# Loop products of an attention kernel cut into 64-row, 32-column TensorE tiles, with the products against V split by row halves into one PSUM bank

## The chip, the cores and the metric

The kernel runs on one core of a Trainium2 chip. The metric is the device time of one execution in microseconds; lower is better. Each time is the median of several executions, and one further execution was recorded by the hardware profiler.

## What is computed

A transformer block with adaptive layer norm on a 2048 x 512 input: attention with 32 query heads of 16 elements that share one key and one value head, then a gated feed-forward layer of width 1792. The core of the reference:

```python
q = (x @ wq).reshape(B, S, H, Dh).transpose(0, 2, 1, 3)      # H = 32, Dh = 16
k = x @ wk
v = x @ wv
scores = jnp.einsum("bhqd,bkd->bhqk", q, k) * (Dh ** -0.5)
p = _softmax(scores, axis=-1)
o = jnp.einsum("bhqk,bkd->bhqd", p, v)                        # then @ wo
...
h = _sigmoid(x @ w_gate) * (x @ w_up)                         # then @ w_down
...
h = _layernorm(x, axis=-1) * (1 + ca) + sa                    # ca, sa, ga, ... from silu(c) @ w_mod
x = x + ga * _A_ref(h, A_wq, A_wk, A_wv, A_wo)
h = _layernorm(x, axis=-1) * (1 + cb) + sb
x = x + gb * _B_ref(h, B_w_gate, B_w_up, B_w_down)
```

## The kernel before

A **prologue** (`PLAN`, a hand-written order) loads the input, normalises it, and makes K (`kp`), V (`V`, fp32, with columns of ones so that row sums come with the product) and the first queries. A **loop** of 512 steps does all attention and seven eighths of the feed-forward layer. A **tail** does the last eighth.

The loop runs over 32 units (`units`: 8 blocks of 256 queries, each with 4 groups of 8 heads), and in each over 16 blocks of 128 keys. The query tile `qp` holds head pairs twice, in partitions 0 to 63 and 64 to 127 (index `j`), so score products have a contraction of 64 rows and two of them can stand in the two row halves of the TensorE array at once. A step s holds:

- four **`sa`** products (`a_tile`): scores with queries on the partitions, 64 x 128 tiles with 512 columns, for the row maxima. Each goes to one of three PSUM banks, and `a_max` on VectorE (DVE) reduces it into `mx`. They run about 1.3 units ahead (`A0 = 84`), since a unit's maxima enter its `qp` as two more rows (`max_rows`).
- four **`st`** products (`st_tile`): scores with keys on the partitions, 64 x 128 tiles with 512 columns, in one of two banks; ScalarE (ACT) takes the exponential into `P`.
- one **`pv`** for step s - 2 (`LAG`): four fp32 products of `V` (128 rows, 32 columns) with `P`, side by side in the four column groups of the array, accumulated over the unit's 16 steps in the one bank `c`. Where no side product is running, `pv` is cut into two halves of 256 columns at two places of the step.
- **side products**: queries (`pq`), the output projection (`po`), gate and up (`pgu`, 256 columns), down (`pd`), in fp16 with hi and lo parts. `Couple` runs two groups at once, one in each row half, and swaps the halves in the middle so that each group sees all 128 rows. `plan`, `places` and `piece` deal a couple's terms into three places of a step, `RATE = 4.5` terms a step.

The order on TensorE, VectorE and ScalarE in the loop is the order of the code (`keep_in_program_order`). The step's skeleton:

```python
scores(0); piece() or light(s); scores(1)      # scores(n): st_tile, then a_tile
pv(*vq[0], None if full else 0)
scores(2); piece(); scores(3)
if not full: pv(*vq[0], 1)
piece()
```

`unit_end` copies the finished bank `c` to `cs`, on DVE for all but the first four units.

Of the kernel before, what the change touches and what calls it, by code (L numbers as in the profile page):

```python
# [22 lines left out]
QB = 512  # L23
# [3 lines left out]
NKB = S // P  # L27
# [29 lines left out]
LAG = 2  # L57
# [4 lines left out]
SKIP = 9  # L62
GAP = 2
KEPT = 2
RATE = 4.5
MOST = 6
WSTEPS = 110
WLAST = 112
WLATE = 2
WSTORE = 5  # L70
QPLAIN = 3
FIRST = 75
QLEAD = 6
W1 = 2
# [10 lines left out]
def adaln_mqa_glu_kernel(  # L85
# [34 lines left out]

    def sbank(name):
        return psum["s"].tile([P, 512], F32, tag=name, name=name, bufs=psum["banks"][name])

    def cbank(name):
        return psum["c"].tile([P, 512], F32, tag="c", name=name, bufs=1)


    class Ordered:
        def __init__(self, engine):
# [9 lines left out]

    class Group:
        def __init__(self, stage, n, name, term, end, begin=None, w=1):
# [17 lines left out]
    class Couple:  # L162
# [3 lines left out]
        def part(self, n0, n1):  # L166
            if n0 == 0:
                for g in self.gs:
                    g.open()
            m = self.gs[0].n  # L170
            for n in range(n0 * self.w, n1 * self.w):
                for j in range(2):
                    g = self.gs[j ^ (n >= m)]
                    l_, r_, *cut = g.term(n % m, slice(64 * j, 64 * j + 64))
                    pe.matmul(g.bank[:, cut[0]] if cut else g.bank, l_, r_, start=(n == 0), stop=(n == 2 * m - 1))
            if n1 == self.n:
                for k, g in enumerate(self.gs):
                    g.end(g.bank, k == 1)
# [366 lines left out]
    def a_product(i, n):  # L545
        qp = get_q(i)
        if i not in mxs:
            mxs[i] = wp.tile([P, 8, 2, 4], F32, tag="mx", name="mx", bufs=2)
        kc, qt, j, r = spot(n)
        sa = sbank("sa")  # L550
        pe.matmul(sa, qp[64 * j:64 * j + 64, r, qt * P:(qt + 1) * P],
                  kp[64 * j:64 * j + 64, kc * 512:(kc + 1) * 512], start=True, stop=True)
        return i, n, sa

    def a_max(i, n, sa):
        kc, qt, j, r = spot(n)
        dve.tensor_reduce(mxs[i][:, 4 * j + r, qt, kc:kc + 1], sa, axis=AX.X, op=ALU.max)
        if i > 0 and n == 63:
            pend.append((i,))

    def a_tile(i, n):
        a_max(*a_product(i, n))
# [26 lines left out]

    def st_tile(i, t, pr, j):  # L590
        qp = get_q(i)
        if j == 0:
            P_["p"] = P2.tile([P, 2, 512], F32, tag=f"P{pr}", name=f"P{pr}", bufs=PBUFS)
        p_ = P_["p"]
# [8 lines left out]
    def pv(i, t, half=None):  # L603
        if t == 0 and half != 1:
            Cs[i] = cbank("c")
        cut = slice(0, QB) if half is None else slice(half * QB // 2, (half + 1) * QB // 2)
# [3 lines left out]
        if half == 0:  # L610
            return
        for hh in range(4):
            del Ps[i, t, hh]
        if t == NKB - 1:
            unit_end(i)

    def unit_end(i):
        b, o = units[i]
        cs = t32("cs")
        if pinned and b > 0:  # L620
            dve.tensor_copy(cs, Cs.pop(i))
        else:
            act.activation(cs, Cs.pop(i), AF.Identity)
        if i == len(units) - 1:
            last.append(cs)
            return
        lD = dr.tile([2, 8, QU], F32, tag="lD", name="lD", bufs=3)
        raw = t32("raw")
        defer(1, lambda: place(b, o, cs, lD, raw))
# [288 lines left out]
    first.clear()  # L918
    pctx.close()
    psum["ctx"].close()  # L920
    psum["c"] = ctx.enter_context(tc.tile_pool(name="pc", bufs=1, space=PSUM, reuse_waits="tile"))
# [18 lines left out]
    main, spare = [], early[QPLAIN:]  # L940
    run = []
    lead = [0.0]

    def places(m, n):
        skip = 3 * (n - n // 2) - 1
        res = [3 if k + 1 == skip else (1, 2, 1)[k % 3] for k in range(3 * n)]
        for ks in (range(skip), range(skip + 1, 3 * n)):
            order = sorted(ks, key=lambda k: ((0, 2, 1)[k % 3], k))  # L950
            while sum(res[k] for k in ks) != m:
                d = 1 if sum(res[k] for k in ks) < m else -1
                res[order[0]] += d
                order.append(order.pop(0))
        res[skip] = 0
        return res

    def pick(s):
        while main and main[0][0] is None:
# [13 lines left out]
        return spare.pop(0) if spare else None  # L973


    def plan(s):
        if s < FIRST:
            return None
        if not run:
            g = pick(s)  # L980
            if g is None:
                lead[0] = 0.0
                return None
            if g.stage == "tr":
                n, sizes = 1, [2, 0, 2]
            else:
                least = -(-g.n // MOST)
                n = min(max(least, round((g.n + lead[0]) / RATE)), len(units) * NKB - s)
                if n < least:
                    spare.insert(0, g)  # L990
                    return None
                sizes = places(g.n // 2, n)
            at = 0
            for k, z in enumerate(sizes):
                run.append((g, at, at + z, n if k == 0 else 0))
                at += z
        lead[0] += sum(z[2] - z[1] for z in run[:3]) - RATE
        return "run"

    def piece():  # L1000
        if run:
            g, n0, n1, _ = run.pop(0)
            if n1 > n0:
                g.part(n0, n1)


    def light(s):
        c_, n = divmod(s, 25)
        if c_ < QPLAIN and n < 24:
            early[c_].part(n, n + 1)  # L1010

    vq = []
    before = None

    for i, (b, o) in enumerate(units):
        if o == 0 and b > 0:
# [3 lines left out]
        for kb in range(NKB):  # L1020
            s = i * NKB + kb
            now[0] = s
            if kb == NKB - QLEAD - 5 and i + 2 < len(units):
                get_q(i + 2)
            late, pend[:] = pend[:], []
            for z in [z for z in waits if z[0] <= s]:
                waits.remove(z)
                z[1]()
            rows = [max_end(*z) for z in late]
            an = A0 + 4 * s  # L1030

            def scores(n):
                st_tile(i, kb, n // 2, n % 2)
                if an + (n ^ 1) < len(alist):
                    a_tile(*alist[an + (n ^ 1)])

            scores(0)
            if before == "run":
                piece()
            else:  # L1040
                light(s)
            scores(1)
            now_ = plan(s)
            full = now_ is not None
            if len(vq) >= LAG:
                pv(*vq[0], None if full else 0)
            lows = [z() for z in rows]
            scores(2)
            if now_ == "run":
                piece()  # L1050
            scores(3)
            if len(vq) >= LAG:
                if not full:
                    pv(*vq[0], 1)
                vq.pop(0)
            if now_ == "run":
                piece()
            for z in lows:
                z()
            before = now_  # L1060
            vq.append((i, kb))
            while wdone < nw:
                if wdone < nw - 4 and (wdone + 0.5) * WSTEPS > (s + 1) * (nw - 4):
                    break
                if wdone >= nw - 4 and s < WLAST + 3 * (wdone - nw + 4):
                    break
                wjobs[wdone]()
                wdone += 1
    assert wdone == nw and len(qdone) == 4 * NB
    while run:  # L1070
        piece()
    while vq:
        pv(*vq.pop(0))
    while waits:
        now[0] += 1
        for z in [z for z in waits if z[0] <= now[0]]:
# [52 lines left out]
```

## Time and profile before

| | |
|---|---|
| median of 3 runs (lowest to highest) | 1710.07 us (1707.37 to 1710.59) |
| the profiled execution: its time, its span | 1709.06 us, 1707.3 us |
| busy TensorE matmul / VectorE / ScalarE / GpSimd | 1671.2 / 1423.2 / 1249.9 / 635.0 us |
| matmuls in the profile | 16204 |
| granted TensorE clock | 0.995 |

In the profile's rows PE is TensorE's matmuls, PEld its weight loads, and a form such as `64*128 64x512 f16` is a tile of 64 rows and 128 columns with 512 moving columns. One fp32 product stands in the profile as two load and matmul pairs. Matmuls are pipelined and their ends are modelled, so the distance between starts tells how long a product takes, and the duration of a row is that plus a pipeline's length.

### The profile page before, as it was taken

To read this page: it belongs to the slowest core of one execution; us is meant where nothing else is said; L and a number is where in the kernel's file an instruction comes from. 1 tells how busy PE (TensorE), PEld (TensorE's weight loads), DVE (VectorE), ACT (ScalarE), POOL (GpSimd) and SP (SyncE) were. 2 spreads that over 40 slices of the span, in tenths; PEclk is the share of its full clock that TensorE was granted. 3 is DMA by queue.
4 is the path that set the end of the run, shared out by engine and by line. 5 is a ranking of instruction groups with operands and counts; after the bars stand their busy time and mean duration, and the time that the engine had idled before them with its cause. 6 is when DMAs were issued, how large, how long until landed. Compare 5 with 4: busy or idle time off the path is not lost.

```text
span 1707.3 us, 40077 instructions
## 1 busy us (share of the span) xinstructions
PE 1671.2 (98%) x16204; PEld 702.5 (41%) x16204; DVE 1423.2 (83%) x2390; ACT 1249.9 (73%) x2309; POOL 635.0 (37%) x831
## 2 busy tenths in 40 slices
PE   6999999999999999999999999999999999999998
PEld 3323333344433443344433443344433443334565
DVE  7899999989889998988988998989889888993121
ACT  5559888777777777777777777777777777787500
POOL 4433544765515332342324331432324232232233
PEclk9989999999999999999999999999999999999999
DMA  7112333433102210121102210122003210122222
GB/s 234 68 49 75 99 105 99 136 97 116 46 22 76 86 62 13 50 96 61 33 23 88 73 62 26 37 96 64 29 24 99 65 60 13 36 81 69 81 99 72
DMA packets 92549, 120.35 MB, mean 70 GB/s; under 512 B 23764, under 2 KB 64716, under 8 KB 92364
## 3 DMA queue, kind: packets, MB, share of 16 engines
q1 hardware_dynamic: 92364, 117.80, 21.3%
q8 instruction: 127, 2.08, 0.5%
q14 instruction: 58, 0.48, 0.1%
HBM read 97.18 MB, written 16.24 MB: 66 GB/s over the span
## 4 chain that ended last, share of the span: by engine, by line
PE 90%; DVE 3%; ACT 3%; POOL 1%; DMA 1%; SPq 1%; issue 1%; POOLq 0%; ACTq 0%; DVEq 0%
PE c L134 29%; PE st L134 21%; PE pgu L134 15%; PE sa L134 9%; PE pd L134 6%; PE pgu L158 3%; PE pd L158 2%; PE po L134 2%; PE pq L134 2%; DVE mx L134 2%; ACT P L134 1%; DMA xall<-in_A_x_dram 1%; DVE st L134 1%; SPq L134 0%; PE pt L134 0%
## 5 line engine op out<-in xcount | busy, mean ns | idle before, releaser
L134 DVE TENSOR_REDUCE mx<-sa 128x1 f32<-128x512 f32 x2048 | 1294.3, 682 | 133.5 <-PE sa L134 125.7
L134 ACT ACTIVATE P<-st 128x512 f32<-128x512 f32 x2048 | 1137.5, 595 | 304.3 <-PE sa L134 258.1
L134 PE MATMUL sa<-kp,qp 64*128 64x512 f16 x2048 | 755.5, 383 | 4.9 <-DVE mx L134 4.7
L134 PE MATMUL st<-qp,kp 64*128 64x512 f16 x2048 | 755.3, 380 | 3.8 <-ACT P L134 2.5
L134 PE MATMUL c<-P,V 128*32 128x512 f32 (+1 forms) x4744 | 562.3, 546 | 0.3
L134 PE MATMUL pgu<-h,gw 64*128 64x256 f16 x4608 | 374.2, 269 | 2.8 <-POOL h L321 2.8
L134 PEld LDWEIGHTS <-kp 64*128 64x128 f16 x2048 | 184.1, 94 | 467.6 <-issue 415.8
L134 PEld LDWEIGHTS <-gw 64*128 64x128 f16 x4608 | 228.0, 94 | 97.1 <-issue 6.0
L134 PEld LDWEIGHTS <-qp 64*128 64x128 f16 x2048 | 187.1, 93 | 117.9 <-issue 56.1
L831 POOL TENSOR_SCALAR th<-th 128x512 f32<-128x512 f32 x48 | 29.8, 620 | 403.5 <-ACT th L134 392.9
L134 PEld LDWEIGHTS c<-P,V 128*32 128x32 f32 x4744 | 93.5, 108 | 159.0 <-issue 149.6
L521 POOL MEMSET qp<- 32x1024 f16 x60 | 56.7, 945 | 77.0 <-PE st L134 74.5
L285 POOL TENSOR_SCALAR wst<-wst 128x512 f32<-128x512 f32 x46 | 28.6, 621 | 136.1 <-DMA wst<-in_B_w_up_dram 51.8
L134 DVE COPY u<-pgu 128x512 f32<-128x512 f32 x48 | 32.6, 680 | 44.4 <-PE pgu L134 25.7
L837 POOL TENSOR_TENSOR gl<-th,gh 128x512 f16<-128x512 f32 x56 | 64.8, 1158 | 4.7
L134 PE MATMUL pd<-wdh,gl 64*128 64x512 f16 x336 | 63.8, 376 | 0.0
L134 PE MATMUL pd<-wdl,gh 64*128 64x512 f16 x336 | 63.8, 376 | 0.0
L134 PE MATMUL pd<-wdh,gh 64*128 64x512 f16 x336 | 63.7, 376 | 0.0
L859 POOL TENSOR_TENSOR ot<-ot,gb 128x512 f32<-128x512 f32 x12 | 15.2, 1270 | 129.7 <-ACT ot L134 129.7
L832 POOL TENSOR_TENSOR th<-th,u 128x512 f32<-128x512 f32 x48 | 60.9, 1270 | 4.0
L662 POOL TENSOR_TENSOR raw<-raw 128x256 f32<-128x256 f32 x31 | 22.6, 730 | 104.8 <-DMA raw<-lD 80.8
L836 POOL TENSOR_SCALAR gh<-th 128x512 f16<-128x512 f32 x56 | 34.8, 621 | 41.2 <-DVE th L834 37.0
(155 smaller groups left out, 1122.5 us busy)
## 6 DMA issues: line engine op xcount, KB each, us to landing
gw<-wD SPq DMA_DIRECT2D x112, 512.0 KB
wD<-gw SPq DMA_DIRECT2D x14, 512.0 KB
wm<-in_w_mod_dram SPq DMA_DIRECT2D x6, 1024.0 KB
qp<-qD SPq DMA_DIRECT2D x192, 32.0 KB
qD<-q SPq DMA_DIRECT2D x16, 256.0 KB
xr<-in_A_x_dram SPq DMA_DIRECT2D x16, 256.0 KB
out_dram<-ot SPq DMA_DIRECT2D x16, 256.0 KB
raw<-cs SPq DMA_DIRECT2D x248, 16.0 KB
```

The costliest lines, as they stand in the source:

```text
L134: return (lambda *a, **k: keep(f_(*a, **k))) if pinned else f_
L158: pe.matmul(self.bank[:, cut[0]] if cut else self.bank, l_, r_, start=(n == 0), stop=(n == self.n - 1))
L285: pool.tensor_scalar(w_, w_, SW, 0.0, op0=ALU.mult, op1=ALU.add)
L521: eng.memset(qp[j:j + 32], 0.0)
L662: keep(pool.tensor_tensor(raw[:, :QU], raw[:, :QU], raw[:, QU:], op=ALU.mult))
L831: pool.tensor_scalar(th, th, 1.0, 1.0, op0=ALU.add, op1=ALU.mult)
L832: pool.tensor_tensor(th, th, u_, op=ALU.mult)
L836: pool.tensor_scalar(hi, th, 1.0, 0.0, op0=ALU.mult, op1=ALU.add)
L837: pool.tensor_tensor(lo, th, hi, op=ALU.subtract)
L859: pool.tensor_tensor(ot, ot, mods[5], op=ALU.mult)
```

## The change

Every product of the loop, but for the small transposes and the maxima's rows, is now cut into tiles of 64 rows and 32 columns: a product that was one 64 x 128 tile is four 64 x 32 tiles with the same moving operand (`columns`). `pv` is cut into row halves too: for each row half `j` and each half of the columns, four fp32 products of 64 rows. Both row halves add into the same bank, `c`, now a fixed PSUM tensor (`craw`) outside the pools' bookkeeping. [...] 

A step now has two half-steps h. In half-step h row half h works on V, and the other half on two `sa` and two `st` products; one piece of the side products stands at its end. `light` and the second kind of step go; `plan` and `places` deal terms by half-step (`RATE = 2.2`, in the early part `QRATE = 0.9`). The copy of bank `c` to `cs` is always on ACT. In the prologue the pool `sa` has 3 banks in place of 4, since `craw` holds one from the start.

```diff
-RATE = 4.5
-MOST = 6
+RATE = 2.2
+QRATE = 0.9
+MOST = 3
+SWAP = 5
...
+    raw_c = {"c": nc.alloc_psum_tensor("craw", [P, 512], F32).ap()}
...
-    psum["n"], psum["banks"] = 4, {"sa": 4}
+    psum["n"], psum["banks"] = 4, {"sa": 3}
...
+    def columns(dst, l_, r_, start, stop):
+        for c_ in range(0, P, 32):
+            pe.matmul(dst[c_:c_ + 32], l_[:, c_:c_ + 32], r_, start=start, stop=stop)
...
+    def hand_over():
+        g, rs = 32 * (done[0] // 2 % 4), slice(64 * side[0], 64 * side[0] + 64)
+        z = pe.matmul(raw_c["c"][g:g + 32, 0:1], nought[rs], nought[rs, 0:1], start=False, stop=False)
...
+        done[0] += 1
+        z.then_inc(turn, 1)
...
+    def take_over():
+        pe.wait_ge(turn, done[0])
...
             for n in range(n0 * self.w, n1 * self.w):
+                if n == m:
+                    take_over()
                 for j in range(2):
...
-                    pe.matmul(g.bank[:, cut[0]] if cut else g.bank, l_, r_, start=(n == 0), stop=(n == 2 * m - 1))
+                    columns(g.bank[:, cut[0]] if cut else g.bank, l_, r_, n == 0, n == 2 * m - 1)
+                if n == m - 1 and open_[0]:
+                    hand_over()
...
-        pe.matmul(s_, kp[64 * j:64 * j + 64, t * P:(t + 1) * P], qp[64 * j:64 * j + 64, 2 * pr:2 * pr + 2].rearrange("p r q -> p (r q)"),
-                  start=True, stop=True)
+        columns(s_, kp[64 * j:64 * j + 64, t * P:(t + 1) * P], qp[64 * j:64 * j + 64, 2 * pr:2 * pr + 2].rearrange("p r q -> p (r q)"),
+                True, True)
...
+    def pv(i, t, j, half):
+        c_ = raw_c["c"]
+        side[0] = j
+        cut, rs = slice(half * QB // 2, (half + 1) * QB // 2), slice(64 * j, 64 * j + 64)
+        if half == 0 and (t, j) != (0, 0):
+            take_over()
         for hh in range(4):
-            pe.matmul(Cs[i][32 * hh:32 * hh + 32, cut], V[:, t, :], Ps[i, t, hh][:, cut],
-                      start=(t == 0 and half != 1), stop=(t == NKB - 1 and half != 0))
+            z = pe.matmul(c_[32 * hh:32 * hh + 32, cut], V[rs, t, :], Ps[i, t, hh][rs, cut],
+                          start=(t == 0 and j == 0 and half == 0), stop=(t == NKB - 1 and j == 1 and half == 1))
...
+        open_[0] = (t, j, half) != (NKB - 1, 1, 1)
+        if half == 1 and open_[0]:
+            hand_over()
...
-        if pinned and b > 0:
-            dve.tensor_copy(cs, Cs.pop(i))
-        else:
-            act.activation(cs, Cs.pop(i), AF.Identity)
+        raw_c["out"] = act.activation(cs, raw_c["c"], AF.Identity)
...
+            for h in range(2):
+                for k in range(2):
+                    if an + 2 * k + 1 - h < len(alist):
+                        a_tile(*alist[an + 2 * k + 1 - h])
+                    if len(vq) >= LAG:
+                        pv(*vq[0], h, k)
+                    st_tile(i, kb, k, 1 - h)
...
+                piece(s, h)
```

TensorE in the middle of the loop, before: two score products, one whole `pv` (four rows), and two score products again. `gl`, `gh`, `wdl` and `wdh` belong to a down projection that runs beside them.

```order
L134 MATMUL pd<-wdh,gl 128x512
L134 LDWEIGHTS kp
L134 MATMUL st<-qp,kp 128x512
L134 LDWEIGHTS qp
L134 MATMUL sa<-kp,qp 128x512
L134 MATMUL c<-P_10716,V 32x512
L134 MATMUL c<-P_10735,V 32x512
L134 MATMUL c<-P_10716,V 32x512
L134 MATMUL c<-P_10735,V 32x512
L134 LDWEIGHTS kp
L134 MATMUL st<-qp,kp 128x512
```

TensorE in the middle of the loop, now: the end of one `sa` product's four tiles, the second half of the columns of one row half of `pv`, the product with zeros that hands the bank over, and the first tile of an `st` product in the other row half.

```order
L132 LDWEIGHTS qp
L132 MATMUL sa<-kp,qp 32x512
L132 MATMUL craw<-P_35473,V 32x256
L132 MATMUL craw<-P_35491,V 32x256
L132 MATMUL craw<-P_35473,V 32x256
L132 MATMUL craw<-P_35491,V 32x256
L132 LDWEIGHTS nought
L132 MATMUL craw<-nought 32x1
L132 LDWEIGHTS kp
L132 MATMUL st<-qp,kp 32x512
```

The output's first number went from 128 to 32 in `sa` and `st`, and the columns of a V product from 512 to 256; the list of TensorE's instructions went from 24,844 rows to 94,013.

VectorE at the end of a unit, before, with the copy of bank `c` between the maxima:

```order
L134 TENSOR_TENSOR mh<-m_5117,mh 16x128
L134 TENSOR_REDUCE mx<-sa 128x1 x22
L134 COPY cs<-c 128x512
L134 TENSOR_REDUCE mx<-sa 128x1 x3
L134 COPY u<-pgu 128x512
```

ScalarE at the end of a unit, now, with that copy between the exponentials:

```order
L132 ACTIVATE P_4080<-st 128x512
L132 ACTIVATE P_4098<-st 128x512
L132 ACTIVATE P_4080<-st 128x512
L132 ACTIVATE cs<-craw 128x512
L132 ACTIVATE P_4098<-st 128x512
```

The copy left VectorE's list and stands in ScalarE's, one exponential later than the end of the unit.

More of the change, by code (lines that the diff above doesn't have):

```diff
@@ L550, in a_product @@
         sa = sbank("sa")
-        pe.matmul(sa, qp[64 * j:64 * j + 64, r, qt * P:(qt + 1) * P],
-                  kp[64 * j:64 * j + 64, kc * 512:(kc + 1) * 512], start=True, stop=True)
+        l_, r_ = qp[64 * j:64 * j + 64, r, qt * P:(qt + 1) * P], kp[64 * j:64 * j + 64, kc * 512:(kc + 1) * 512]
+        if first:
+            pe.matmul(sa, l_, r_, start=True, stop=True)
+        else:
+            columns(sa, l_, r_, True, True)
         return i, n, sa
@@ L619, in unit_end @@
         cs = t32("cs")
-        if pinned and b > 0:
-            dve.tensor_copy(cs, Cs.pop(i))
-        else:
-            act.activation(cs, Cs.pop(i), AF.Identity)
+        raw_c["out"] = act.activation(cs, raw_c["c"], AF.Identity)
+        behind(raw_c["out"], raw_c["last"])
+        tc.declare_no_dep(raw_c["out"].ins, group="turn", reason="later matmuls into the bank stand for them")
         if i == len(units) - 1:
@@ L939, in adaln_mqa_glu_kernel, with weight, places @@
     early = [Couple(q_group(*z), q_group(*y)) for z, y in zip(qleft[::2], qleft[1::2])]
-    main, spare = [], early[QPLAIN:]
+    main, spare = [], early
     run = []
     lead = [0.0]
[L946 to L956, printed above, removed]
+    def weight(hb, q):
+        s, h = divmod(hb, 2)
+        t = (s - LAG) % NKB
+        if s >= LAG and (t, h) == (0, 0):
+            return 0.0
+        if (t, h) == (NKB - 1, 1):
+            return SWAP / RATE if not q else 1.0
+        return 1.0 if q else (2 - SWAP / RATE + 2 * (NKB - 1)) / (2 * NKB - 2)
+    def places(m, hb, rate, most, skip):
+        ws = []
+        while sum(ws) * rate < m + lead[0] - rate / 2 or sum(ws) * most < m:
+            ws.append(0.0 if len(ws) < skip else weight(hb + len(ws), rate == QRATE))
+        lead[0] += m - rate * sum(ws)
+        ends = [round(m * sum(ws[:k + 1]) / sum(ws)) for k in range(len(ws))]
+        return [k - z for z, k in zip([0] + ends, ends)]
     def pick(s):
@@ L973, in pick, with plan, piece @@
         return spare.pop(0) if spare else None
[L976 to L1000, printed above, removed]
-        if run:
-            g, n0, n1, _ = run.pop(0)
+    def plan(s, hb):
+        if run:
+            return
+        g = pick(s)
+        if g is None:
+            lead[0] = 0.0
+            return
+        if g.stage == "tr":
+            sizes = [4]
+        else:
+            q = g.stage == "q" and s < FIRST
+            rate, most = (QRATE, 1) if q else (RATE, MOST)
+            sizes = []
+            for leg in range(2):
+                sizes += places(g.n // 2, hb + len(sizes), rate, most, 3 if q and leg == 0 else 0)
+            if hb + len(sizes) > 2 * len(units) * NKB:
+                spare.insert(0, g)
+                return
+        at = 0
+        for z in sizes:
+            run.append((g, at, at + z))
+            at += z
+        assert at == g.n, (at, g.n, g.stage)
+    def piece(s, h):
+        plan(s, 2 * s + h)
+        if run:
+            g, n0, n1 = run.pop(0)
             if n1 > n0:
                 g.part(n0, n1)
[L1007 to L1010, printed above, removed]
     vq = []
-    before = None
+    lows = []
     for i, (b, o) in enumerate(units):
@@ L1030, in adaln_mqa_glu_kernel @@
             an = A0 + 4 * s
[L1032 to L1044, printed above, removed]
-            if len(vq) >= LAG:
[L1046 to L1054, printed above, removed]
-                vq.pop(0)
[L1056 to L1060, printed above, removed]
+            old, lows[:] = lows[:], []
+            for h in range(2):
[5 more added lines that the diff above has]
+                    st_tile(i, kb, k, 1 - h)
+                if h == 1:
+                    lows.extend(z() for z in rows)
+                piece(s, h)
+                if h == 0:
+                    for z in old:
+                        z()
+            if len(vq) >= LAG:
+                vq.pop(0)
             vq.append((i, kb))
@@ L1070, in adaln_mqa_glu_kernel @@
     while run:
-        piece()
+        piece(s, 1)
     while vq:
-        pv(*vq.pop(0))
+        for n in range(4):
+            pv(*vq[0], n // 2, n % 2)
+        vq.pop(0)
     while waits:
```

42 lines of the change are left out of this document (24 added, 18 removed).

## The prediction

> **What bounds the kernel now.** The page's first two parts come first, then the chain that ended last.
>
> ```profile
> PE 1671.2 (98%) x16204; PEld 702.5 (41%) x16204; DVE 1423.2 (83%) x2390; ACT 1249.9 (73%) x2309; POOL 635.0 (37%) x831
> PE 90%; DVE 3%; ACT 3%; POOL 1%; DMA 1%; SPq 1%; issue 1%; POOLq 0%; ACTq 0%; DVEq 0%
> PE c L134 29%; PE st L134 21%; PE pgu L134 15%; PE sa L134 9%; PE pd L134 6%; PE pgu L158 3%; PE pd L158 2%; PE po L134 2%; PE pq L134 2%; DVE mx L134 2%; ACT P L134 1%; DMA xall<-in_A_x_dram 1%; DVE st L134 1%; SPq L134 0%; PE pt L134 0%
> ```
>
> TensorE is busy 98% and holds 90% of the chain. Next the groups that write `c` and `cs`, and the busy time (and instructions) of PE, PEld, DVE, ACT and POOL between 108 and 1608 us:
>
> ```profile
> 108.00:1608.00 1500.00, 1491.77 (x15023) 604.81 (x15023) 1312.50 (x2174) 1190.82 (x2212) 550.28 (x696) 1.00 0.20 65
> L134 PE MATMUL c<-P,V x4744: 379/592/617, 109.7 to 1610.1; 128*32 128x512 f32 x145, 128*32 128x256 f32 x53
> L134 DVE COPY cs<-c x28: 679/692/693, 315.1 to 1610.8; 128x512 f32<-128x512 f32 x28
> ```
>
> The first `c` product starts at 109.7 us and the last at 1610.1, so the window is the loop: 1500 us, 2.93 us for each of 512 steps; PE is busy 1491.77, DVE 1312.5 (0.875), ACT 1190.82. Next, TensorE's timeline in one step: start, duration, product.
>
> ```profile
> 700.05 0.38 PE L134 MATMUL po<-wol,a 64*128 64x512 f16 x2
> 700.27 0.38 PE L134 MATMUL po<-woh,a 64*128 64x512 f16 x2
> 700.48 0.38 PE L134 MATMUL sa<-kp,qp 64*128 64x512 f16 x1
> 700.49 0.38 PE L134 MATMUL st<-qp,kp 64*128 64x512 f16 x1
> 700.79 1.07 PE L134 MATMUL c<-P,V 128*32 128x512 f32 x8
> 701.79 0.39 PE L134 MATMUL st<-qp,kp 64*128 64x512 f16 x1
> ```
>
> Products of one shape follow each other every 0.215 us, two at a time in the two row halves. But `c` starts 0.09 us after `sa` is through (700.48 + 0.215 = 700.70), and the next product comes 1.00 us after `c` began. How much of this is streaming shows at the end of the loop, where several `c` products stand in a row:
>
> ```profile
> 1608.34 2.36 PE L134 MATMUL c<-P,V 128*32 128x256 f32 x24
> 1610.63 0.39 PE L158 MATMUL po<-woh,a 128*128 128x512 f16 x1
> ```
>
> These 24 records are six waves of four, two of 256 columns and four of 512: ten half waves and one change of shape in 2.29 us. Eight records above are four half waves and a change in 1.00. The difference gives 0.215 us for a half wave, and 0.14 for the change at the end. With the 0.09 ahead, a visit to `c` loses 0.23 us in which the array drains.
>
> **What the change removes.** The visits are counted by shape.
>
> ```profile
> L134 PE MATMUL c<-P,V 128*32 128x512 f32 x3448 | 459.0, 604 | 0.0
> L134 PE MATMUL c<-P,V 128*32 128x256 f32 x1296 | 103.5, 391 | 0.3
> L134 PE MATMUL pgu<-h,gw 64*128 64x256 f16 x4608 | 374.2, 269 | 2.8 <-POOL h L321 2.8
> ```
>
> Whole visits have 8 records and half visits 8: 3448/8 + 1296/8 = 431 + 162 = 593. With one tile shape for the loop none of them should drain: **-593 x 0.23 = -136 us**. That it is the shape and not fp32 against fp16 that drains is an assumption, since the two always change together here.
>
> The array's streaming stays the same. A 64 x 128 product becomes four tiles of a quarter of its width, each as long; a `c` record becomes four, half as high and half as long. So PE's step becomes (1500 - 136)/512 = 2.66 us before anything is added.
>
> **What it adds.** *Hand-overs.* 1062 products with zeros; each holds one tile of eight for a few columns, costed at nothing. What counts is the wait. In TensorE's queue behind a `take_over` stand the `pv` half, the next `st`, the side piece, and by them ACT and DVE; ahead of it stand, mostly, four tiles of `st`, a piece and four of `sa`, 0.215 us + 2.2 x 0.215 on both halves, and these cover it. A row's 0.38 us against its 0.215 of streaming says that a result is 0.17 us later than its last column; with the semaphore I bound a wait without cover between 0 and 0.25 us. The new order has some 72 couples, each with two bare waits around its swap (only four tiles between): 144 x 0.17 = **+24 us**, bounds 0 and 36. Some 80 more stand in half-steps without a piece, mostly where DVE sets the pace: 0, at most +20.
>
> *VectorE and ScalarE come close.* The reduces pile up where PE gives many:
>
> ```profile
> 1493.71 4.84 DVE L134 TENSOR_REDUCE mx<-sa 128x1 f32<-128x512 f32 x8
> 1498.47 0.68 DVE L134 BATCH_NORM_STATS2 st<-xr 128x6 f32<-128x512 f32 x1
> L134 DVE TENSOR_REDUCE mx<-sa 128x1 f32<-128x512 f32 x2048 | 1294.3, 682 | 133.5 <-PE sa L134 125.7
> L134 ACT ACTIVATE P<-st 128x512 f32<-128x512 f32 x2048 | 1137.5, 595 | 304.3 <-PE sa L134 258.1 <-PE st L134 15.7 <-PE pgu L134 9.1
> L134 ACT ACTIVATE cs<-c x4: 598/603/604, 149.0 to 272.2; 128x512 f32<-128x512 f32 x4
> ```
>
> Eight in 4.76 us: 0.595 each, 2.38 us a step at the least, and some 0.1 for the rest, against PE's 2.71 with the hand-overs. So DVE does not take over, but its load goes from 0.875 to (1312 - 19)/1388 = 0.93, where 19 us are the 28 copies of `cs` that leave it. ACT takes these at 0.60 each, 1208/1388 = 0.87. The next unit's first `pv` waits for that copy; side products of 5 terms, 1.07 us, are dealt there, so nothing. In-order PE stops at each `sa` whose bank DVE still holds, and holds up `pv` and `st` behind it. Some 120 steps have a further 0.68 us operation on DVE; with a slack of 0.23 us a step each could cost up to 0.45: bounds 0 and 54, I take **+30 us**, the middle.
>
> *The prologue* has one `sa` bank fewer: bounds 0 and 5, **+1**. The tail is the same.
>
> *Instructions.* Loads and matmuls in the loop go from 2 x 15,023 in 1500 us (50 ns each) to some 2 x 58,000, 12 ns each. The trace shows such a rate only in bursts. Below are the fetches of instructions, the values' products in the chain, the first and the last of their 48 rows in TensorE's timeline, and a row of loads:
>
> ```profile
> q8 instruction: 127, 2.08, 0.5%
> 59.29 1.30 PE pv L134 x48
> 59.22 0.18 PE L134 MATMUL pv<-wkvh,h1h 128*128 128x16 f16 x1
> ...
> 60.41 0.17 PE L134 MATMUL pv<-wkvh,h1l 128*128 128x16 f16 x1
> 1117.97 0.16 PEld L134 LDWEIGHTS c<-P,V 128*32 128x32 f32 x8 [0.24 <-issue]
> ```
>
> 47 distances in 1.19 us: 25.3 ns for a load and a matmul, in one tile, where each waits for its own load. Across tiles it is faster: eight loads of 0.106 us or more begin within 0.05 us, 7 ns apart. Both may have been queued before. I take 0, since 25 ns is the limit of one tile and eight tiles share the new load; the upper bound is a rival below.
>
> *Loads in a column tile.* The ten half waves at 0.215 us stand in one tile shape, each with a load of its own for the next, and no time between them. [...]
>
> **Sum.** 1709 (the profiled execution; the median is 1 above it) - 136 + 24 + 30 + 1 = 1628, so a median of **1629 us**.
>
> **The rivals.**
>
> *Instruction supply (slower).* If TensorE's front end cannot sustain more than the 25.3 ns a pair of the row above, the place is the steps beside `pgu`, whose 256 columns stream in half the time for the same instructions. A step there has 32 pairs of `pv`, 16 of `sa`, 16 of `st`, 2 of hand-overs and 70 of the piece (4.4 terms of 16), 136 in all: 3.44 us. Such steps are 4608 x 4/70 = 263; the other 249, with about 101 pairs (2.56 us), keep 2.7. 263 x 3.44 + 249 x 2.7 = 1577, 77 more than 1500: 1786. It decides from about 23 ns a pair on (263 x 136 x 0.023 + 249 x 2.7 = 1495). For it: no long stretch of the trace runs at that rate, and the fetches of instructions (127 packets now) grow 3.6 times with it. Against: the 7 ns. **22%.** [...]
>
> *DVE holds what PE gives up.* `DVE mx` waits 125.7 us for `sa` now. If half of the drained time turns into waits of PE for `sa` banks, -68 + 24: about 1665. **12%.**
>
> *Hand-overs bare throughout.* If nothing covers the wait, 1062 x 0.17 = 181 in place of 24: 1786; at 0.25, 1870. It decides from 0.1 us each. Against: the piece between. **8%.**
>
> *The drains stay.* If fp32 beside fp16 drains the array, four alternations in each of 1024 half-steps at 0.1 us and more, and V could not run beside `sa` and `st`: over 2100. For it: every drain in the trace has both changes. Against: `sa` began at 700.48 ahead of `st` at 700.49, though `st` stands first in the order, so tiles run on their own. **4%.** *Nothing comes of it*, gain and costs even: **4%**.
>
> **How the numbers follow.** The forecast has the remaining 50%, with a range of its own from 1709 - 136 = 1573 (all costs 0) to 1573 + 36 + 20 + 54 + 5 = 1688. A difference under 0.2% (3.4 us) cannot be told from none. Faster: 50 + 12 = 62%; same 4%; slower 22 + 8 + 4 = 34%. For 8 in 10 the range must take in the supply rival and the hand-overs at 0.17: 1575 to 1800.
>
> **What would show it.** Right: matmuls on `craw` that start within some 10 ns of `sa` and `st` tiles, no gap of 0.1 us before or after them, a step of 2.7 us, DVE over 0.9 in the loop. The supply rival shows as steps beside `pgu` of 3.4 us with TensorE's rows 25 ns apart and DVE and ACT waiting for PE, the other steps faster than now. Bare hand-overs show as PE waiting 0.2 us before each first `craw` product of a half. Drains show as gaps around every one. The forecast is wrong if the loop takes over 1500 us, or if PE is idle while it waits for DVE by more than 60 us.

## The result, and the profile after

The changed kernel takes 2024.7 us (median of 4, 2022.39 to 2033.53), the kernel before 1709.71 (median of 4 beside them, 1707.37 to 1710.59): 1.185 times as long, 95% interval 1.182 to 1.189. It is slower by 315 us where the forecast had it faster by 80, and outside the range. The profiled execution took 2024.46 us, its span is 2022.5.

The profile page of the changed kernel, parts 1 (its first line), 3 (fetches of instructions) and 4 (the chain):

```profile
PE 1736.2 (86%) x59518; PEld 1189.6 (59%) x59518; DVE 1422.5 (70%) x2362; ACT 1254.7 (62%) x2337; POOL 634.4 (31%) x832
q8 instruction: 465, 7.62, 1.6%
PE 78%; issue 12%; DVE 3%; POOL 2%; ACT 2%; DMA 1%; SPq 1%; POOLq 0%; ACTq 0%; DVEq 0%
```

TensorE falls from 98% to 86% of a longer span, and "issue", time in which an engine waits for nothing that the profile shows, goes from 1% to 12% of the chain, some 240 us. The fetches, the packets of the q8 queue, grow from 127 to 465. VectorE and ScalarE, which the forecast feared, fall to 70% and 62%: the view of waits (us, times, longest us) shows them waiting for TensorE, and TensorE waiting for "issue".

```profile
ACT P L132 <- PE st L132: 452.1, 671, 9.1
DVE mx L132 <- PE sa L132: 405.3, 522, 9.1
PEld L132 <- issue: 350.1, 526, 3.6
PE pgu L132 <- issue: 103.7, 119, 3.4
```

The mechanism of the change works. This is TensorE's timeline of a half-step beside `pd`:

```profile
1000.48 0.39 PE L132 MATMUL sa<-kp,qp 64*32 64x512 f16 x4
1000.49 0.39 PE L132 MATMUL craw<-P,V 64*32 64x256 f32 x4
1000.69 0.39 PE L132 MATMUL st<-qp,kp 64*32 64x512 f16 x4
1000.71 0.39 PE L132 MATMUL craw<-P,V 64*32 64x256 f32 x4
1000.91 0.39 PE L132 MATMUL sa<-kp,qp 64*32 64x512 f16 x4
1000.92 0.39 PE L132 MATMUL craw<-P,V 64*32 64x256 f32 x4
...
1001.36 0.16 PE L132 MATMUL craw<-nought 64*32 64x1 f16 x1
...
1001.77 0.39 PE L132 MATMUL craw<-P,V 64*32 64x256 f32 x4
```

V's products start within 0.02 us of `sa` and `st` in the other row half and follow each other every 0.215 us, without the 0.23 us around a visit to `c`; the next half's V products start 0.41 us after the zeros, behind a piece (`hand_over`'s product with zeros raises the semaphore `turn`, for which the other half's first product waits in `take_over`; a couple's swap does the same). From 1000.48 to 1001.77 a half-step takes 1.29 us: 2.58 a step, under the forecast's 2.71, though steps like this one take 2.94 on average (table below). And 560 us earlier, beside `pgu`, these rows stand among the others:

```profile
438.50 0.41 PE L132 MATMUL pgu<-h,gw 64*32 64x256 f16 x14 [1.14 <-issue]
...
442.52 0.41 PE L132 MATMUL pgu<-h,gw 64*32 64x256 f16 x16 [1.21 <-issue]
...
446.27 0.40 PE L132 MATMUL pgu<-h,gw 64*32 64x256 f16 x12 [0.75 <-issue]
...
450.44 0.16 PE L132 MATMUL craw<-nought 64*32 64x1 f16 x1 [1.36 <-issue]
```

In these rows TensorE stands still every 3.75 to 4.2 us for about a microsecond, at whatever instruction is next. When all of TensorE's instructions are numbered in the order of their starts, those on semaphores too, the stops lie 256 apart: of the distances over 0.3 us between two starts in the loop some 314 fall on the same place modulo 256, and on no other place are there more than 4. So 256 instructions are called a page below; a q8 packet has 16384 bytes, and there is one packet for each 256 of TensorE's instructions (465 for 119,209). Over the loop's 456 pages the distances at this place add up to some 340 us. The q8 records time a fetch: in the stops of over 0.7 us, some 230, the packet (counted along with the pages) starts a median 1.18 us after TensorE's first instruction of the page before, takes 1.09 us, and the first instruction of its own page comes 1.40 us after it landed (1.19 to 1.67). That is some 3.7 us from page to page; the earliest of these packets starts 0.57 us after that first instruction. In the kernel before a page lasted 12.7 us (118 in the 1500 us of the loop), and at no place modulo 256 do the distances of its loop add up to more than some 9 us.

For what follows the loop is cut into steps (from every fourth `P<-st` of ScalarE to the fourth next), each counted by the side product in it; the numbers are worked out from the traces. An instruction is a load or a matmul of TensorE, an fp32 product being two of each.

| kernel | time, us | beside `pgu`: steps, instructions, us | beside `pd`, `po`, `pq`: instructions, us |
|---|---|---|---|
| before | 1709.7 | 255, 68, 3.02 | 50, 2.86 |
| changed | 2024.7 | 262, 269, 4.08 | 188, 2.94 |
| e1_merged | 1878.8 | 264, 237, 3.62 | 156, 2.87 |
| e5_zeros | 2217.8 | 265, 300, 4.49 | 220, 3.35 |
| e6_even | 1844.9 | 317, 205, 3.20 | 170, 3.08 |
| e7_halfmax | 1866.5 | 264, 237, 3.58 | 157, 2.85 |
| e12_early | 1930.9 | 262, 237, 3.64 | 156, 3.08 |
| e13_banks | 1875.7 | 264, 234, 3.60 | 153, 2.82 |
| e14_banks_early | 1930.2 | 265, 234, 3.63 | 153, 3.03 |
| e15_halfexp | 1850.8 | 264, 234, 3.54 | 153, 2.78 |

### The profile page after: what moved, and what is told of

The parts are those of the page before. It is cut to its first block, busy times and chain, and to the rows that moved or that the text cites. A ratio compares the mean times of both kernels' runs of the same rounds, so it can differ in the third digit from the quotient of the medians.

```text
span 2022.5 us, 127438 instructions
## 1 busy us (share of the span) xinstructions
PE 1736.2 (86%) x59518; PEld 1189.6 (59%) x59518; DVE 1422.5 (70%) x2362; ACT 1254.7 (62%) x2337; POOL 634.4 (31%) x832
## 4 chain that ended last, share of the span: by engine, by line
PE 78%; issue 12%; DVE 3%; POOL 2%; ACT 2%; DMA 1%; SPq 1%; POOLq 0%; ACTq 0%; DVEq 0%
PE craw L132 25%; PE pgu L132 16%; PE sa L132 13%; PE st L132 8%; PE pd L132 7%; DVE mx L132 2%; PE po L132 2%; PE pq L132 2%; PE pgu L183 2%; PE pd L183 2%; SPq L132 1%; ACT P L132 1%; POOL ot L903 1%; DMA xall<-in_A_x_dram 1%; POOL h L350 0%
## 5 line engine op out<-in xcount | busy, mean ns | idle before, releaser
L132 PE MATMUL craw<-P,V 64*32 64x256 f32 x16384 | 1166.2, 383 | 58.4 <-issue 55.4
L132 PE MATMUL sa<-kp,qp 64*32 64x512 f16 (+1 forms) x7940 | 867.3, 381 | 35.1 <-issue 20.5
L132 PE MATMUL st<-qp,kp 64*32 64x512 f16 x8192 | 866.9, 383 | 29.8 <-issue 27.6
L132 PEld LDWEIGHTS craw<-P,V 64*32 64x32 f32 x16384 | 502.1, 107 | 206.1 <-issue 100.0
L132 PE MATMUL pgu<-h,gw 64*32 64x256 f16 x18432 | 442.4, 273 | 117.5 <-issue 103.7
L132 PEld LDWEIGHTS <-gw 64*32 64x32 f16 x18432 | 325.3, 92 | 207.2 <-issue 157.5
L132 PEld LDWEIGHTS <-kp 64*32 64x32 f16 x8192 | 310.1, 91 | 93.6 <-issue 53.8
L132 PEld LDWEIGHTS <-qp 64*32 64x32 f16 (+1 forms) x7940 | 276.2, 93 | 123.3 <-issue 84.5
L132 PE MATMUL craw<-nought 64*32 64x1 f16 x1062 | 173.9, 164 | 6.6 <-issue 6.6
L132 PEld LDWEIGHTS <-nought 64*32 64x32 f16 x1062 | 99.4, 94 | 42.1 <-issue 15.0
```

Source lines behind the costliest of these rows:

```text
L132: return (lambda *a, **k: keep(f_(*a, **k))) if pinned else f_
```

## Experiments

The theory: the fetch of TensorE's instructions, a page of 256 at a time, sets the steps. Its rivals: a slow front end that issues instructions evenly, stops at the hand-overs, and VectorE and ScalarE.

**e4_burst: what a page costs by itself.** Ahead of the loop:

```
+    for n in range(3071):
+        zero(n % 4)
+    for n in range(1024):
+        zero(0)
...
+    for n in range(2048):
+        pe.wait_ge(turn, 1)
```

`zero(g)` is a load and a product of one column in the 64 x 32 tile number `g`.

> The changed kernel with three bursts ahead of the loop, in which TensorE waits for nothing: 3072 pairs of a load and a one-column matmul over four tiles of 64 x 32 in turn (24 pages), 1024 such pairs in one tile (8 pages), and 2048 waits on a semaphore that is already there (two to an instruction, 4 pages). Instruction fetch: 3.7 us a page whatever the instruction, so 89, 30 and 15 us, with stops of 1 to 2.5 us every 256 instructions; the whole about 2155 us. Rival (a rate of the front end): evenly spaced instructions with no stops; at the 5 ns an instruction seen in the densest stretches 31 us for the first burst, and 26 us for the second by 25.3 ns a pair.

TensorE's timeline in the first two bursts:

```profile
113.59 1.18 PE L132 MATMUL craw<-nought 64*32 64x1 f16 x128 [2.67 <-issue]
117.32 1.18 PE L132 MATMUL craw<-nought 64*32 64x1 f16 x128 [2.55 <-issue]
121.05 1.18 PE L132 MATMUL craw<-nought 64*32 64x1 f16 x128 [2.54 <-issue]
...
195.07 2.10 PE L132 MATMUL craw<-nought 64*32 64x1 f16 x128 [2.82 <-issue]
198.80 7.02 PE L132 MATMUL craw<-nought 64*32 64x1 f16 x256 [1.63 <-issue]
```

Exactly 128 products, 256 instructions, run in about 1.02 us, 4 ns each, and then nothing runs for 2.3 to 2.8 us. From 113.59 to 195.07 are 22 pages: 3.70 us a page, 14.5 ns an instruction, 28.9 a pair. That is not the rival's even rate: within a page an instruction starts every 4 ns, and then none does. In one tile a pair takes 7.02/256 = 27.4 ns, nearly the page's 28.9, and behind the row at 198.80 no stop is over 0.43 us. The expectation for the third burst missed: a wait that is already met costs TensorE 0.108 us (110.6 us for 1025 instructions, in place of 15), and the kernel took 2240 in place of 2155.

**e1_merged: fewer instructions, the same array work.**

```
-        cut, rs = slice(half * QB // 2, (half + 1) * QB // 2), slice(64 * j, 64 * j + 64)
...
+        cut, rs = slice(0, QB), slice(64 * j, 64 * j + 64)
...
-                    if len(vq) >= LAG:
-                        pv(*vq[0], h, k)
+                    if k == 1 and len(vq) >= LAG:
+                        pv(*vq[0], h)
```

> The changed kernel with the two 256-column halves of each V product of a row half issued as one of 512 columns: the same array work and the same 1062 hand-overs, 8192 pairs of a load and a matmul fewer. Theory (instruction fetch): a page of 256 TensorE instructions cannot follow the page before it in under about 3.7 us, and the loop is 456 such pages; 64 pages go, 64 x 3.7 = 237 us, so about 1790 us (1760 to 1830). Rival (hand-overs stop TensorE): their number stays, so 2000 to 2040. Rival (VectorE and ScalarE set the pace): 2000 to 2040.

1878.8 us, 1.0996 (1.093 to 1.106) of the kernel before and 146 us under the changed one, with as many hand-overs. That is less of a gain than the theory's 1760 to 1830, and more than the 2000 to 2040 of both rivals. The page of the profile has

```profile
q8 instruction: 401, 6.57, 1.5%
```

64 packets less. The stops at the page's place go from some 340 us to 152. Steps beside `pgu` lose 32 instructions and 0.46 us, 14.4 ns for each. Beside the others only 0.07 goes: there the fetch was hardly the limit any more, and the expected 237 us had counted every page as one that stops. The edit also moves the first half of V's products behind the third score tile; e12 below shows that their place matters too, so e5 is the cleaner test.

**e5_zeros: more instructions.**

```
         if half == 1 and open_[0]:
+            for n in range(8):
+                g = 32 * (n % 4)
+                pe.matmul(c_[g:g + 32, 0:1], nought[rs], nought[rs, 0:1], start=False, stop=False)
             hand_over()
```

> The changed kernel with eight more products of zeros, of one column each, ahead of each hand-over of V's bank: 8192 pairs, 64 pages more, which take 4 ns an instruction where they are at hand (the first burst), 66 us at the most. Instruction fetch at 14.5 ns an instruction: a step beside pgu has 32 more instructions and takes 0.46 us more, a step beside pd, po or pq goes from 188 to 220, 3.19 us, 0.25 more; 262 x 0.46 + 225 x 0.25 = 177, so about 2200 us (2170 to 2270). Rival (only the array or the waits count): 2025 to 2090.

2217.8 us, 1.296 (1.292 to 1.300) of the kernel before, 193 more than the changed kernel and inside the expected 2170 to 2270. The page of the profile has

```profile
q8 instruction: 527, 8.63, 1.6%
```

62 packets more, and the stops at the page's place grow from some 340 us to 474. These products of one column cost 0.40 us a step beside `pgu` and 0.41 beside the others, 13 ns an instruction. Beside the others 0.25 was expected; whether the zeros also delay the hand-over behind them there was not separated. The time follows the number of instructions up and down.

**e6_even: the same instructions, dealt more evenly.**

```
-            rate, most = (QRATE, 1) if q else (RATE, MOST)
+            rate, most = (QRATE, 1) if q else (1.65, MOST) if g.stage == "gu" else (3.3, 4)
```

> e1_merged with pgu dealt at 1.65 terms a half-step and the other side products at 3.3, in place of 2.2 for all: the same instructions, spread more evenly over the steps. Instruction fetch, page by page: a step beside pgu has some 102 pairs in place of 120, 2.96 us; 349 of them, 120 others at 3.26 by the array, 43 without: 1535, and with the 0.16 us a step that e1's steps lie above the fetch 1590 in place of 1667: about 1800 us (1770 to 1840). Rival (what counts is the number of instructions in all, or the hand-overs): 1870 to 1890.

On e1_merged: 1844.9 us, 34 less, at as many instructions. The steps beside `pgu` do fall, to 3.20 us at 205 instructions, but there are 317 of them and the others rise to 3.08. Of the expected 80 us less than half came. The stops at the page's place are down to 96 us; without any of them this kernel would still take some 1749, an estimate that lets nothing else come in their place. By this estimate the fetch is not all that keeps it above the kernel before.

**e2_64 and e3_128: wider tiles for all but V.** In `columns`, which the score and side products use:

```
-        for c_ in range(0, P, 32):
-            pe.matmul(dst[c_:c_ + 32], l_[:, c_:c_ + 32], r_, start=start, stop=stop)
+        for c_ in range(0, P, 64):      # e3_128: 128
+            pe.matmul(dst[c_:c_ + 64], l_[:, c_:c_ + 64], r_, start=start, stop=stop)
```

> The changed kernel with every loop product but V's on tiles of 64 rows and 64 columns: array work and hand-overs as before it, about 37,700 pairs in the loop in place of 58,000, 295 pages. Instruction fetch: 295 x 3.7 = 1090 us is no longer a bound, nor is a step beside pgu (85 pairs, 170 instructions, 2.46 us); if two tile widths side by side do not drain the array, the loop is what the prediction had without supply, 1388 to 1480, and the time 1600 to 1690 us. If each change of width drains 0.23 us, eight changes a step give more than 2025. Rival (hand-overs or VectorE and ScalarE): 2000 to 2040.

> The changed kernel with every loop product but V's on tiles of 64 rows and all 128 columns, as in the kernel before; V's stay at 64 x 32 with the hand-overs. About 27,600 pairs, 216 pages, 800 us of fetch: no bound. If the width alone does not drain the array, 1600 to 1690 us; if it drains at each of eight changes a step, 0.1 to 0.23 us each, 1388 + 512 x 8 x 0.1 to 0.23 = 1800 to 2330 for the loop, 2000 to 2540 in all. Rival (hand-overs or VectorE and ScalarE): 2000 to 2040.

3054.0 and 3011.9 us, the shorter of two runs each (the others took 3177.0 and 3073.2); for e3_128 2540 was the most that was expected. TensorE's timeline of e3_128:

```profile
1003.47 0.38 PE L132 MATMUL sa<-kp,qp 64*128 64x512 f16 x1
1003.78 0.64 PE L132 MATMUL craw<-P,V 64*32 64x256 f32 x8
1004.24 0.16 PE L132 MATMUL craw<-nought 64*32 64x1 f16 x1
1004.35 0.39 PE L132 MATMUL st<-qp,kp 64*128 64x512 f16 x1
```

V's products start 0.31 us after `sa`, 0.09 behind its last column, as in the kernel before, and `st` starts 0.11 behind the zeros: nothing runs beside V, whose products then hold one row half while the other is idle. So here the width alone, with rows and data types as they were, brings the drains of 0.09 and 0.11 us; the changed kernel's fp32 beside fp16 at one width starts 0.01 us apart (1000.48 and 1000.49 above). Part of these two times is the clock: windows of e3_128 (in the run of 3073.2 us; length, then busy time and instructions of PE, PEld, DVE, ACT, POOL, then the granted clock) show it at 0.50 early in the loop and at 1.00 later, where its steps still take some 5.1 us. In e2_64 it is 0.80 on average from 109 to 1700 us.

```profile
200.00:700.00 500.00, 499.76 (x2888) 103.28 (x2888) 178.68 (x267) 160.23 (x275) 85.79 (x108) 0.50 0.11 33
1200.00:1700.00 500.00, 500.00 (x5641) 194.65 (x5637) 285.06 (x432) 251.31 (x433) 93.76 (x115) 1.00 0.11 33
```

**e7_halfmax: VectorE.**

```
-        dve.tensor_reduce(mxs[i][:, 4 * j + r, qt, kc:kc + 1], sa, axis=AX.X, op=ALU.max)
+        dve.tensor_reduce(mxs[i][:, 4 * j + r, qt, kc:kc + 1], sa if first else sa[:, :256], axis=AX.X, op=ALU.max)
```

> e1_merged with VectorE's reduces in the loop over 256 of the 512 columns (half of the work for the row maxima is left out, and the exponent is scaled down so that it stays finite). Steps beside pd, po or pq take 2.87 us in e1_merged, though their instructions would arrive in 2.28. If VectorE's hold on the sa banks makes the difference to the forecast's 2.71, they fall to 2.6 to 2.75 us and the time to 1835 to 1860; steps beside pgu stay at 3.5 to 3.6. If not, nothing moves: 1870 to 1885.

The kernel leaves out half of the row maxima in the loop, and scales the exponent by 0.02 for 0.25 so that it stays finite. A reduce takes 424 ns for 684. 1866.5 us, 12 less than e1_merged, whose own two runs lie 9 apart; beside `pd`, `po` and `pq` 2.85 us for 2.87, where 2.6 to 2.75 was expected if VectorE held them. It does not.

**e11_turns: a bare hand-over.** Ahead of the loop 256 times, with the row halves in turn:

```
+        take_over()
+        z = pe.matmul(raw_c["c"][g:g + 32, 0:1], nought[rs], nought[rs, 0:1], start=True, stop=True)
+        done[0] += 1
+        z.then_inc(turn, 1)
```

> The changed kernel with 256 hand-overs in a row ahead of the loop: a product of zeros in one row half, which raises the semaphore, and the other half's waits for it, in turn; nothing is beside them. The forecast's price of a bare hand-over, 0.17 us (0 to 0.25): 44 us for the 256 (0 to 64). Rival: in e9_two a product on V's bank followed 0.40 us behind the zeros' start where nothing stood between: 102 us.

```profile
106.65 61.38 PE L132 MATMUL craw<-nought 64*32 64x1 f16 x256
```

0.240 us each. The forecast's 0.17 was low, its bound of 0.25 held.

**e12_early, e13_banks and e14_banks_early: the place of V's products, and no hand-overs between them.** e12 is e1_merged with V's products behind the first score tile:

```
-                    if len(vq) >= LAG:
-                        pv(*vq[0], h, k)
+                    if k == 0 and len(vq) >= LAG:
+                        pv(*vq[0], h)
```

e13 is e7_halfmax with a bank for each row half's V products; the second bank is taken from `sa`. Its 144 products with zeros, in place of 1062, stand at the couples' swaps. e14 is both.

```
-SBANKS = {"st": 2, "sa": 3}
+SBANKS = {"st": 2, "sa": 2}
...
-        c_ = raw_c["c"]
+        c_ = raw_c["c1" if j else "c"]
...
-        if half == 0 and (t, j) != (0, 0):
-            take_over()
```

> e1_merged with V's products behind the first score tile of a half-step, not behind the third. In e1_merged V's 0.86 us of streaming in one row half begin 0.43 us after the half-step and end behind the other half's four score tiles, so that the piece and the hand-over wait for them. If that is why steps beside pd, po or pq take 2.87 us (2.47 by the array), they fall to 2.5 to 2.65, steps beside pgu only to the fetch of their 237 instructions, 3.46 to 3.6; 225 x 0.28 + 264 x 0.1 = 89: about 1790 us (1775 to 1830). If the hand-overs themselves hold them, whatever the order: 1865 to 1890.

> e7_halfmax with a bank of its own for V's products of each row half, so that nothing is handed over but at the swap of a couple (the second bank comes from sa, 2 in place of 3, and is left out of the sum). If hand-overs hold the steps beside pd, po or pq at 2.85 us, these fall to 2.5 to 2.6 and those beside pgu to the fetch of their 233 instructions, 3.4 to 3.5; 225 x 0.3 + 264 x 0.1 = 94 less than e7_halfmax, about 1775 us. If the order of products or the array holds them: 2.8 to 2.9 and about 1860.

> e13_banks with V's products behind the first score tile. If in e12_early the hand-over came with too little ahead of it (3.08 us beside pd, po or pq), that is gone: 2.5 to 2.6 us, about 1770 in all. If V's place itself costs: 3.0 to 3.1 and about 1910.

1930.9, 1875.7 and 1930.2 us. All three expectations of a gain failed. V early makes the steps beside `pd`, `po` and `pq` longer, 3.08 and, without V's hand-overs, 3.03; without V's hand-overs and with V late they take 2.82 for 2.85. The missing `sa` bank hides little of a gain in the loop: there TensorE's `sa` products wait for VectorE 2.9 us in all, for 2.6 in e7_halfmax. It costs the prologue 19 us (the first V product starts at 132.6 us for 113.7), while the loop, from the first V product to the last, is 9 us shorter. So the hand-overs of V's bank are nearly all covered, as the forecast had it, and the place of V's products is worth some 0.2 us a step.

**e15_halfexp: ScalarE.** On e13_banks:

```
-        act.activation(p_[:, j], s_, AF.Exp, scale=0.02)
+        act.activation(p_[:, j, :256], s_[:, :256], AF.Exp, scale=0.02)
```

V's products take these 256 columns twice; half of the exponentials is left out, and one takes 383 ns for 598.

> e13_banks with ScalarE's exponentials over 256 of the 512 columns; V's products take these 256 columns twice, so that the array's work stays (half of the exponentials is left out). If ScalarE, with 2.56 us of work a step and two st banks, holds the steps beside pd, po or pq at 2.82 us, they fall to the array's 2.47 to 2.6; 225 x 0.28 = 63 less than e13_banks, 1810. If TensorE's own order of products holds them: 2.75 to 2.85 and 1860 to 1880. Steps beside pgu stay at the fetch's 3.4 to 3.6 in both.

1850.8 us; 2.78 beside `pd`, `po` and `pq` (median 2.68), where 2.47 to 2.6 was expected if ScalarE held them. With the columns of VectorE's reduces and ScalarE's exponentials halved and V's hand-overs gone the steps beside `pgu` still take 3.54 us, for 234 instructions of 14.5 ns, 3.39.

**e8_whole, e9_two and e10_one: can the drains be saved otherwise?** e8 is the kernel before with `full = True`, so that no visit to `c` is in halves: 81 visits fewer. e9 and e10 take the side products of e1_merged back to 128 x 128, in one visit per two steps and per step:

```
-                    columns(g.bank[:, cut[0]] if cut else g.bank, l_, r_, n == 0, n == 2 * m - 1)
+                pe.matmul(g.bank[:, cut[0]] if cut else g.bank, l_, r_, start=(n % m == 0), stop=(n % m == m - 1))
```

In e10 the pieces then stand at the end of the step:

```
-                piece(s, h)
+                if h == 1:
+                    piece(s, 0)
+                    piece(s, 1)
```

> The kernel before with every V visit whole (512 columns), none in two halves: 81 visits fewer, 81 x 0.23 = 19 us of drains: about 1690 us. Rival: the whole visits stand in steps without a side product, where the ScalarE or VectorE runs dry in the meantime: 1705 to 1720.

> e1_merged with the side products taken out of the small tiles: each is one product on 128 x 128, and they stand together, one visit for the pieces of two steps, after the second step's score tiles. Some 65 pairs a step, 130 instructions, 1.9 us of fetch. By the array 512 x 2.66 + 256 visits x 0.23 us of drains = 1421 us for the loop, and the V products stay beside sa and st: 1421 + 209 + 10 to 60 for VectorE and ScalarE, which have 3 and 2 banks ahead of a visit of 1.9 us: 1640 to 1690 us, faster than the kernel before. Rival (the visits empty the score banks, ScalarE with 1.2 us of work ahead loses 0.7 us in each): 1421 + 256 x 0.7 + 209 = 1810. Rival (hand-overs are bare without a side piece between them, 1024 x 0.17): 1800.

> As e9_two, with one visit a step: 512 x 2.66 + 512 x 0.23 = 1480 us by the array, the visits half as long (0.94 us and the drain), so that ScalarE's and VectorE's banks outlast them: 1480 + 209 + 0 to 40: 1690 to 1730 us. Rival (hand-overs bare without a side piece between them): one of two a step, 512 x 0.17 = 87 more, 1780. Rival (a width change drains only the smaller part, 0.1 us): 1625 to 1660.

1739.8 (1.016, 1.013 to 1.019), 1964.3 (1.149, 1.148 to 1.151) and 1976.3 us (1.157, 1.155 to 1.159). None beats the kernel before, and each is above every time that was expected for it, the rivals' too (at most 1720, 1810 and 1780). In e9 and e10 it is not the fetch: at no place modulo 256 do the distances add up to more than some 12 us. In e9 the steps without a visit take 2.41 us, near ScalarE's four exponentials of 0.596, and those with one 4.2 to 4.7; its waits are

```profile
ACT P L132 <- PE st L132: 473.5, 561, 9.1
DVE mx L132 <- PE sa L132: 385.2, 246, 8.0
```

where in the kernel before `DVE mx` waited 125.7 for `sa`. That fits visits that empty the score banks, as the rival said, but 1964 is well above its 1810, and where the rest goes was not followed.

## Why the prediction was wrong

*The drains removed, -136.* Right as a mechanism: the timeline shows none, and e2_64 and e3_128 show that it was the shape, which the forecast assumed. What a visit costs the whole kernel is less sure: e8 has 81 visits fewer and takes 30 us more, so 0.23 us a visit does not by itself give the time.

*Instruction supply, 0.* This is the step that failed. "I take 0, since 25 ns is the limit of one tile and eight tiles share the new load" took the 7 ns of a burst for a rate that lasts. The last q8 packet before that burst (1117.97 us) had landed at 1109.11 and the next starts at 1120.29; e4 has the like, 4 ns, and then no instructions for 2.3 to 2.8 us. The limit in e4 is the page: 3.70 us for 256. The fetches' row of the kernel before gives only the transfer, some 1.1 us (0.5% of 16 engines' 1707 us for 127 packets), and with pages of 12.7 us no stops there showed the rest. The stops add up to some 340 us of the 396 by which the forecast fell short. How much of that would come back in other waits is open: no run with the whole loop in small tiles is free of the stops, and e1_merged lost 184 us of them for 146 of time.

*The supply rival, 22%.* The right place (steps beside `pgu`) and sign, the wrong price and cause. With e4's 28.9 ns a pair for 25.3, its own sum is 263 x 136 x 0.0289 + 249 x 101 x 0.0289 = 1034 + 727 = 1761 for the loop, 1709 + 261 = 1970 in all; measured 2025. At 25.3 the other 249 steps seemed free, at 28.9 this sum limits them too, though e1_merged gained only 0.07 us there. The steps beside `pgu` took 4.08 us for the rival's 3.44. And e4 shows no even rate: 4 ns an instruction within a page, 14.5 over 22 pages.

*Hand-overs, +24.* Bare ones cost 0.240 us, so 144 of them 35 us; e13 shows the rest nearly covered (0.03 us a step, 9 us of loop for 918 hand-overs fewer). The rival of bare hand-overs throughout is out. Whether the halves have to take turns at one bank was not shown: no run lets both write it at once.

*VectorE and ScalarE, +30.* Their loads fell, from 83% and 73% of the span to 70% and 62%. Halving the columns of VectorE's reduces in the loop gains 12 us, so the term is no larger than that once TensorE is this slow. What it would be in a kernel without the limit of fetch was not measured.

*Loads in a column tile, 0.* Right: the sum has no term for them, and the V products above follow at 0.215 us with loads of their own.

*What stays open.* Beside `pd`, `po` and `pq` a step takes 2.82 us even without V's hand-overs and with half of the columns on VectorE, and 2.78 with half of them on ScalarE as well, for 2.71 in the forecast, though 153 instructions arrive in 2.2. The place of V's products moves it by 0.2; which wait does so was not found.

## What to carry to other kernels

Count a change's instructions per stretch, not only its array time: in e4 TensorE got 256 instructions per 3.70 us, so by that number, an estimate, smaller tiles could pay here only where 256 instructions carry at least that much streaming. A short burst in these profiles said how fast instructions issue (4 and 7 ns), not how fast they arrive (14.5 ns in e4); the rate that lasts has to come from a stretch of several pages. And the signature was easy to find: "issue" stops on one engine (0.75 to 1.36 us in the rows of the changed kernel, 2.3 to 2.8 in e4), at any instruction, 314 of some 410 over 0.3 us at one place modulo 256.

## What the chip showed unexpectedly

- In e4's first burst a page of 256 TensorE instructions followed the one before in a mean 3.70 us, with nothing else to wait for (22 pages in a row, 3.45 to 4.0 each); within a page an instruction issued every 4 ns. A q8 packet took 1.09 us in the stops of the changed kernel.
- A wait on TensorE for a semaphore that was already there, as an instruction of its own, took 0.108 us in e4, as long as 7 instructions at 14.5 ns.
- A bare hand-over between row halves by semaphore took a mean 0.240 us in e11 (61.2 us for 255).
- Tiles of 64 x 32 and 64 x 128, or 64 x 64, did not run side by side: in e3_128 and e2_64 no V product starts within 0.199 us behind a wider tile, where in the changed kernel 29% of them start within 0.02 us behind a score or side tile. The granted clock was 0.50 from 200 to 700 us in e3_128 and 0.80 from 109 to 1700 us in e2_64 (0.99 in the changed kernel's loop), while TensorE's row shows it busy for 499.76 of the 500 and 1590.80 of the 1591 us. Why was not tried.
